# Attention block on one core: P times V for two key tiles in one burst, and side products in slots after each score pair

## The chip, the cores and the metric

One core of a Trainium2 chip runs the whole program. The metric is the device time of one execution in microseconds (us); the kernel before takes 1757.31 us (median of three runs, 1756.65 to 1758.82).

## The reference

A transformer block on 2048 tokens of width 512: attention with 32 query heads of 16 columns that share one key and one value head, then a gated product (GLU without a nonlinearity), both behind a layer norm whose scale and shift come from a condition vector.

```python
mod = (silu(c) @ w_mod).reshape(c.shape[0], 6, 1, -1)        # sa, ca, ga, sb, cb, gb
h = layernorm(x) * (1 + ca) + sa
q = (h @ wq) per head;  k = h @ wk;  v = h @ wv              # 32 heads of q, one of k and v
p = softmax(einsum("bhqd,bkd->bhqk", q, k) * 16 ** -0.5)
x = x + ga * (einsum("bhqk,bkd->bhqd", p, v) @ wo)
h = layernorm(x) * (1 + cb) + sb
x = x + gb * (((h @ w_gate) * (h @ w_up)) @ w_down)          # 512 -> 1792 -> 512
```

## The kernel before

Attention is done in 32 *units*: a unit is four heads for one block of 512 queries (four blocks, eight units each). Keys come in 16 *key tiles* of 128. The loop over a unit has 32 *steps*; step i treats key tile `kt = i // 2` and head pair `p = i % 2`. Everything is issued by hand in program order, so the order in the code is the order in which each engine works.

A step issues two *pairs* on TensorE. A pair is one score product and one row-max product, which use the two halves of the array's rows (64 rows each) at the same time:

- `qk_exp(u, kt, p, a)`: the score product `sc` (L579, fp16) for this unit into a PSUM bank, and the exponential on ScalarE (L581), which writes half a tile `P`. A tile `P` holds the two heads of one key tile and one `p`. `P` has four buffers.
- `max_half(a)`, which calls `max_mm`: the row maxima are needed before a unit starts, so this runs 38 steps ahead, for a later unit: a product `mx` (L542) into a bank, and a maximum over 512 columns on VectorE (L544). The last 38 steps of the loop have none.

At odd steps follows `pv(u, kt - 1)`: P times V for one key tile (L588), four heads into four column groups of 32, all into one PSUM bank `pv`, in fp32, which the chip runs as two passes: eight matmul records in a profile. This is one *burst*. At the first odd step of a unit the last key tile of the unit before is done, and its result is read by ScalarE (`pv_out`, L594).

At even steps *side products* are issued, from a queue `fill`: products of q for later units (`one`: full-array products, L500, two at a time), and the work on the query block that is finished: the product with wo, transposes (`solo`, L713), gate, up and down products (`duo`, L469). A `duo` runs two product groups at once, each on one half of the array's rows; one place in it, two half products side by side, is called a *slot* here. It has two *turns* of as many slots: in the second turn the groups swap halves. After the second turn the results are read (`post`): the first group's at once, the second's at the next `drain_mids`. How many slots an even step takes is set by `pace` (what is left over what is left of the time to `due`), a `credit` that grows with it, and the bounds `BURST` = 6 and `LEAST` = 4: four to six slots, or none.

PSUM has eight banks: three `mx`, two `sc`, one `pv`, one `misc` and one `spare`. `spare` is a third score bank as long as no `duo` runs (`ps_sc`); a `duo` takes `misc` and `spare`.

After the loop the *tail* does what is left of the side products, and the last query block's.

Of the kernel before, what the change touches and what calls it, by code (L numbers as in the profile page):

```python
# [13 lines left out]
F32 = mybir.dt.float32  # L14
# [5 lines left out]
S, D, H, DH, F = 2048, 512, 32, 16, 1792  # L20
# [16 lines left out]
ONE_WAIT = 3  # L37
RESERVE = 31000.0
TR_GAP = 8
BURST = 6  # L40
LEAST = 4
NHF = 14
V_STEP = 31
M_STEP = 25
# [8 lines left out]
def adaln_mqa_glu_kernel(ctx: ExitStack, tc: tile.TileContext, x_in, wq_in, wk_in, wv_in, wo_in,  # L53
# [45 lines left out]
    xbig = big.tile([128, 6, 2, D], F32, name="xbig", tag="wu")  # L99
    xts = [xbig[:, i] for i in range(6)]  # L100
    for i in range(6, 8):
        xts.append(work.tile([128, 2, D], F32, name="P", tag="P", bufs=4))
    for i in range(8):
        if i == 2:
            nc.sync.dma_start(wmA[:, :, 0:1024], wm_v[:, :, 0:1024])
# [468 lines left out]
    def qk_exp(u, kt, p, a):  # L574
        s = sst[u % 3]
        if (u, kt, p) not in ptl:
            ptl[u, kt, p] = work.tile([128, 2, D], F32, name="P", tag="P", bufs=4)
        t = ps_sc()
        nc.tensor.matmul(t, kst[64 * a:64 * a + 50, kt * 128:(kt + 1) * 128],  # L579
                         s[64 * a:64 * a + 50, p, :], start=True, stop=True)  # L580
        nc.scalar.activation(ptl[u, kt, p][:, a, :], t, AF.Exp)  # L581
# [68 lines left out]
    def wo_work(b):  # L650
        def op(t):
            def f(i):
                ch, term = divmod(i, 3)
                ol, wl = TERMS[term]
                return och[b, ch][:, ol, t * 128:(t + 1) * 128], wo[:, wl, ch, :]
            return f

        def pre(t):
            def f(tag=None):
                load_x(b, t)  # L660
                return ps_misc(tag=tag)
            return f

        def fin(t):
            def f(p):
                if b < NB - 1:
                    x1 = work.tile([128, D], F32, name="x1", tag="x1", bufs=4)
                else:
                    x1 = work.tile([128, D], F32, name="x1p", tag="P", bufs=4)
                nc.vector.scalar_tensor_tensor(x1, p, sca[:, 7:8], xls[b, t], op0=OP.mult, op1=OP.add)  # L670
                x1s[b, t] = x1
                s2 = work.tile([128, 1, 2], F32, name="st2", bufs=5)
                bs = work.tile([128, 6], F32, name="bs", bufs=4)
                nb = work.tile([128, 2], F32, name="nb", bufs=4)
                yt = {}

                def spread():
                    nc.vector.bn_stats(bs, x1)

                def aggr():  # L680
                    nc.vector.bn_aggr(s2[:, 0, :], bs)
                    yt["y"] = rstd_of(s2, 1)
                    nc.gpsimd.tensor_tensor(nb[:, 0:1], s2[:, 0, 0:1], yt["y"], op=OP.mult)
                    nc.gpsimd.tensor_scalar(nb[:, 1:2], nb[:, 0:1], -1.0, 0.0, op0=OP.mult, op1=OP.add)

                def nrm():
                    n2 = work.tile([128, D], F32, name="n2", tag="och", bufs=4)
                    nc.scalar.activation(n2, x1, AF.Identity, bias=nb[:, 1:2], scale=yt["y"])
# [329 lines left out]
    def pace(step):  # L1018
# [7 lines left out]
            most = max(most, (n - kept) / max((due - step) / 2, 1.0))  # L1026
        return most

    def open_gate(step):
        if not fill or (fill[0][1] == "one" and step < cur["wait"]):  # L1030
            return False
        if fill[0][1] == "duo" and NU * NSTEP - step < 2 * -(-fill[0][2][0].n // BURST) + 2:
# [6 lines left out]
    def fill_gap(step):  # L1039


        if cur["gen"] is None:
            if not open_gate(step):
                return
            _, kind, what, due = fill.popleft()
            if kind == "solo":
                _, f, post = what
                credit[0] -= 4.0
                f()
                if post:  # L1050
                    posts.append(post)
                return
            if kind == "one":
                cur.update(gen=plain(what), left=what.n, turn=what.n, second=True, due=due, swapped=-9, one=True)
            else:
                begin(step, what, due)
        if cur["one"]:
            burst(step, max(1, min(int(credit[0]), cur["left"], MOST_ONE)))
            return
        turn = cur["turn"]  # L1060
        parts = max(-(-turn // BURST), min(round(turn / max(credit[0], 1.0)), turn // LEAST), 1)
        n = -(-turn // parts)
        if not cur["second"]:
            n = max(n, -(-cur["turn"] // max((NU * NSTEP - 2 - step) // 2, 1)))
        burst(step, n)

    def begin(step, two, due, tags=("misc", "spare")):
        cur.update(gen=duo(*two, tags=tags), left=2 * two[0].n, turn=two[0].n, second=False, due=due, swapped=-9,
                   one=False)

    def burst(step, n):
        for _ in range(n):
            swap = next(cur["gen"], None)
            credit[0] -= 1.0
            cur["left"] -= 1
            cur["turn"] -= 1
            if swap is None:
                cur["gen"], cur["left"], cur["wait"] = None, 0, step + ONE_WAIT
                return
            if swap:  # L1080
                cur["turn"], cur["second"], cur["swapped"] = cur["left"], True, step
                return

    side = deque(wlist)
# [45 lines left out]
    for u in range(NU):  # L1130
# [3 lines left out]
        for i in range(NSTEP):  # L1134
# [3 lines left out]
            spare["scores"] = not spare["held"] and (cur["gen"] is None or cur["one"]) and not (fill and fill[0][1] == "duo" and open_gate(step))  # L1138
            max_half(0)
            qk_exp(u, kt, p, 1)  # L1140
            drain_mids()
            qk_exp(u, kt, p, 0)
            max_half(1)
            if p == 1:
                if kt == 0:
                    if u > 0:
                        pv(u - 1, KT - 1)
                        posts.append(lambda u=u: pv_out(u - 1))
                else:
# [30 lines left out]

    u = NU - 1

    pv(u, KT - 1)
    pv_out(u)
    left = cur["left"]
    if cur["gen"] is not None:
        assert cur["second"] and NU * NSTEP - cur["swapped"] > 2
        for _ in cur["gen"]:
            drain_posts()
        drain_mids()  # L1190
# [51 lines left out]
```

## Time and profile before

| What | Value |
|---|---|
| Runs | 1756.65, 1757.31, 1758.82 us |
| Span of the profiled execution | 1754.7 us |
| TensorE busy | 1695.0 us, 97% |
| VectorE busy | 1412.2 us, 80% |
| ScalarE busy | 1220.7 us, 70% |
| GpSimd (POOL) busy | 505.0 us, 29% |
| Row maxima on VectorE (L544) | 2048, 682 ns each |
| Exponentials on ScalarE (L581) | 2048, 596 ns each |
| P times V matmul records (L588) | 4096, from 95.9 to 1603.3 us |

The profiled execution's time outside its span isn't listed; the runs' median is 2.6 us above the span. A row of the timeline gives the start in us from the span's start, the length, engine, line, operation, what it writes and reads, and how many are merged (`x2`); in brackets stands the idle time before it and what ended it. Matmuls are pipelined: a record is longer than its share of TensorE, and the distance between starts tells what one costs. In a group's row stand busy time and mean length, then the engine's idle time before, with its releaser.

### The profile page before, as it was taken

The numbers are of one execution on the slowest core, as the hardware profiler recorded it, in microseconds if no ns is written. First come the engines' busy times: TensorE is split into PE (matmuls) and PEld (weight loads), VectorE is DVE, ScalarE is ACT, GpSimd is POOL, SyncE is SP. The second block draws the span as 40 slices with busy tenths as digits, with TensorE's granted clock in tenths as the row PEclk, the third lists the DMA queues.
The fourth block names the chain that finished last, engine by engine and source line by source line (L and its number), as shares of the span: only waits on it lengthen the run. The fifth ranks groups of instructions, "written<-read, shape, count | busy, mean of one in ns | idle before, by whom it ended". The sixth has DMA issues, their size and how long they took to land.

```text
span 1754.7 us, 32145 instructions
## 1 busy us (share of the span) xinstructions
PE 1695.0 (97%) x12655; PEld 540.8 (31%) x12655; DVE 1412.2 (80%) x2363; ACT 1220.7 (70%) x2277; POOL 505.0 (29%) x703
## 2 busy tenths in 40 slices
PE   6899899999999999999999999999999999999999
PEld 3222222222223333333223333333223333324444
DVE  7899899999988888888988888888998899920310
ACT  3478788888777777777787777777787777774210
POOL 5714344646576741100031011100031010110330
PEclk9999999999989999999999999999999999999999
DMA  5202121212222200000100000000100000001000
GB/s 197 101 30 85 52 79 55 89 38 91 81 62 60 69 22 9 5 15 19 41 19 16 9 16 9 5 15 18 51 9 16 9 16 9 11 4 41 19 1 24
DMA packets 48899, 66.58 MB, mean 38 GB/s; under 512 B 15270, under 2 KB 29418, under 8 KB 48748
## 3 DMA queue, kind: packets, MB, share of 16 engines
q1 hardware_dynamic: 47164, 64.33, 11.9%
q8 instruction: 99, 1.62, 0.4%
q14 instruction: 52, 0.43, 0.1%
q10 hardware_dynamic: 1584, 0.20, 0.1%
HBM read 51.12 MB, written 8.92 MB: 34 GB/s over the span
## 4 chain that ended last, share of the span: by engine, by line
PE 83%; ACT 7%; DVE 3%; POOL 3%; DMA 2%; issue 1%; SPq 1%; ACTq 0%; POOLq 0%; DVEq 0%
PE pv L588 27%; PE misc L469 18%; PE mx L542 14%; PE sc L579 13%; PE misc L500 9%; ACT P L581 5%; DVE mpart L544 2%; ACT ev L594 1%; POOL h L395 1%; DMA wmA<-in_w_mod_dram 1%; DMA wsl<-in_B_w_gate_dram 0%; ACT qf L510 0%; DVE x L670 0%; PE mxt L556 0%; PE misc L252 0%
## 5 line engine op out<-in xcount | busy, mean ns | idle before, releaser
L544 DVE TENSOR_REDUCE mpart<-mx 128x1 f32<-128x512 f32 x2048 | 1296.1, 682 | 135.8 <-PE sc L579 117.3
L581 ACT ACTIVATE P<-sc 128x512 f32<-128x512 f32 x2048 | 1102.2, 596 | 320.8 <-PE sc L579 311.7
L542 PE MATMUL mx<-kst,sst 48*128 48x512 f16 x2048 | 649.7, 385 | 15.3 <-DVE mpart L544 12.2
L579 PE MATMUL sc<-sst,kst 50*128 50x512 f16 x2048 | 631.7, 383 | 20.9 <-ACT P L581 17.6
L588 PE MATMUL pv<-P,vst 128*32 128x512 f32 x4096 | 552.0, 611 | 0.0
L542 PEld LDWEIGHTS <-sst 48*128 48x128 f16 x2048 | 156.0, 94 | 574.9 <-issue 519.2
L469 PE MATMUL misc<-h2T,wu 64*128 64x512 f16 x1008 | 253.5, 375 | 0.0
L469 PE MATMUL misc<-h2T,wg 64*128 64x512 f16 x1008 | 253.5, 375 | 0.0
L763 POOL TENSOR_SCALAR glu<-gf 128x512 f16<-128x512 f32 x56 | 34.7, 620 | 544.7 <-DVE gf L762 544.7
L579 PEld LDWEIGHTS <-kst 50*128 50x128 f16 x2048 | 138.3, 94 | 80.1 <-issue 40.5
L588 PEld LDWEIGHTS pv<-P,vst 128*32 128x32 f32 x4096 | 81.1, 108 | 173.6 <-issue 168.5
L469 PEld LDWEIGHTS <-wu 64*128 64x128 f16 x1008 | 94.6, 94 | 57.5
L469 PEld LDWEIGHTS <-wg 64*128 64x128 f16 x1008 | 94.3, 94 | 52.4 <-issue 0.9
L762 DVE TENSOR_TENSOR gf<-misc,g 128x512 f32<-128x512 f32 x56 | 38.2, 683 | 86.8 <-PE misc L500 62.9
L469 PE MATMUL misc<-wd,glu 64*128 64x512 f16 x840 | 105.8, 375 | 0.0
L621 POOL TENSOR_TENSOR oc<-oc,rr 128x512 f32<-128x512 f32 x15 | 19.1, 1277 | 257.7 <-DMA sst<-qd 154.2
L756 ACT ACTIVATE g<-misc 128x512 f32<-128x512 f32 x56 | 33.5, 598 | 69.1 <-PE misc L500 63.4
L764 POOL TENSOR_TENSOR glu<-gf,glu 128x512 f16<-128x512 f32 x56 | 64.8, 1157 | 4.7
L469 PEld LDWEIGHTS <-glu 64*128 64x128 f16 x840 | 43.6, 94 | 45.7 <-issue 1.7
L500 PE MATMUL misc<-wd,glu 128*128 128x512 f16 x252 | 55.1, 379 | 0.0
L500 PE MATMUL misc<-h,wq 128*128 128x512 f16 x168 | 51.2, 387 | 0.0
L848 POOL TENSOR_TENSOR kwb<-kwb,wsl 128x448 f32<-128x448 f32 (+1 forms) x40 | 47.5, 1188 | 3.1
(230 smaller groups left out, 886.7 us busy)
## 6 DMA issues: line engine op xcount, KB each, us to landing
wsl<-in_B_w_gate_dram SPq DMA_DIRECT2D x32, 224.0 KB
wsl<-in_B_w_up_dram SPq DMA_DIRECT2D x32, 224.0 KB
wsl<-in_B_w_down_dram SPq DMA_DIRECT2D x28, 256.0 KB
sst<-qd SPq DMA_DIRECT2D x186, 32.0 KB
qd<-q SPq DMA_DIRECT2D x16, 256.0 KB
oc<-ev SPq DMA_DIRECT2D x128, 32.0 KB
rr<-ri SPq DMA_DIRECT2D x16, 256.0 KB
xl<-in_A_x_dram SPq DMA_DIRECT2D x16, 256.0 KB
```

The source lines that it names most:

```text
L469: nc.tensor.matmul(p, left[64 * r:64 * r + 64], right[64 * r:64 * r + 64], start=start, stop=stop)
L500: nc.tensor.matmul(p, left, right, start=i == 0, stop=i == g.n - 1)
L542: nc.tensor.matmul(m, s[64 * a:64 * a + 48, p, t * 128:(t + 1) * 128], kst[64 * a:64 * a + 48, kc * 512:(kc + 1) * 512], start=True, stop= ...
L544: nc.vector.tensor_reduce(mparts[u][:, a, p, t, kc:kc + 1], m, axis=AX.X, op=OP.max)
L579: nc.tensor.matmul(t, kst[64 * a:64 * a + 50, kt * 128:(kt + 1) * 128], s[64 * a:64 * a + 50, p, :], start=True, stop=True)
L581: nc.scalar.activation(ptl[u, kt, p][:, a, :], t, AF.Exp)
L588: nc.tensor.matmul(pvb[u][32 * j:32 * j + 32, :], vst[:, kt, :], ptl[u, kt, p][:, a, :], start=(kt == 0), stop=(kt == KT - 1))
L756: nc.scalar.activation(st["g", f], p, AF.Copy, scale=2.0 ** -45)
L762: nc.vector.tensor_tensor(gf, p, st["g", f], op=OP.mult)
L763: nc.gpsimd.tensor_scalar(st["glu"][:, 0, f, :], gf, 1.0, 0.0, op0=OP.mult, op1=OP.add)
L764: nc.gpsimd.tensor_tensor(st["glu"][:, 1, f, :], gf, st["glu"][:, 0, f, :], op=OP.subtract)
L848: nc.gpsimd.tensor_tensor(acc, acc, t, op=OP.add)
```

## The change

- At every fourth step (`i % 4 == 1`) `pv` is called for two key tiles in a row, kt-2 and kt-1; at the first such step of a unit for the last two key tiles of the unit before. Products so start a key tile later, and `P` has six buffers.
- `fill_gap` becomes `fill_slot`, called after each pair except the one ahead of a burst: seven places between two bursts (numbered 0 to 6). `plan` spreads a turn of a `duo` over these places, or over those of several bursts, so that it ends at a burst. A new `duo` begins two steps after the last at the earliest, at one of the first four places. Products of q and transposes are issued at places 1 and 5.
- `drain_mids` (reading the second group's result) moves from the middle of each step to just ahead of a burst.

```diff
-BURST = 6
-LEAST = 4
+SLOTS = 7
+SLOT_MOST = 3
+CREDIT = 9.0
+DUO_WAIT = 2
...
-            ptl[u, kt, p] = work.tile([128, 2, D], F32, name="P", tag="P", bufs=4)
+            ptl[u, kt, p] = work.tile([128, 2, D], F32, name="P", tag="P", bufs=6)
...
+    def plan(step, k):
+        rate = max(2 * pace(step), 1.0)
+        part = (SLOTS - k) / SLOTS
+        n = max(0, round((cur["turn"] - credit[0]) / rate - part))
+        if part < 0.5 and cur["turn"] > SLOT_MOST * (SLOTS - k):
+            n = max(n, 1)
+        last = (END - 3 - step) // 4
+        cur["slots"] = SLOTS - k + SLOTS * (min(n, last) if not cur["second"] else n)
+
+    def fill_slot(step, k):
...
+        if cur["slots"] == 0:
+            if k == 0 or (step - 2) // 4 == (cur["swapped"] - 2) // 4:
+                return
+            plan(step, k)
+        n = cur["turn"] // cur["slots"]
+        cur["slots"] -= 1
         burst(step, n)
...
             qk_exp(u, kt, p, 1)
-            drain_mids()
+            fill_slot(step, 2 * ((i - 2) % 4))
             qk_exp(u, kt, p, 0)
             max_half(1)
-            if p == 1:
-                if kt == 0:
-                    if u > 0:
-                        pv(u - 1, KT - 1)
-                        posts.append(lambda u=u: pv_out(u - 1))
-                else:
+            if i % 4 == 1:
+                drain_mids()
+                if kt > 0:
+                    pv(u, kt - 2)
                     pv(u, kt - 1)
+                elif u > 0:
+                    pv(u - 1, KT - 2)
+                    pv(u - 1, KT - 1)
+                    posts.append(lambda u=u: pv_out(u - 1))
                 late_max()
-            elif fill or cur["gen"]:
-                credit[0] = min(credit[0] + pace(step), 9.0)
-                one = cur["one"] if cur["gen"] else fill[0][1] == "one"
-                if credit[0] >= (MOST_ONE if one else 1.0):
-                    fill_gap(step)
+            else:
+                fill_slot(step, 2 * ((i - 2) % 4) + 1)
```

TensorE's order in unit 7, where no side products run, around a burst (`P` is the tile of exponentials, `sst` the queries, `kst` the keys). Before:

```order
L579 LDWEIGHTS kst_124
L579 MATMUL sc_5361<-sst1_120,kst_124 128x512
L542 LDWEIGHTS sst2_122
L542 MATMUL mx_5364<-kst_124,sst2_122 128x512
L588 MATMUL pv_5187<-P_5301,vst_117 32x512 x2
L588 MATMUL pv_5187<-P_5327,vst_117 32x512 x2
L542 LDWEIGHTS sst2_122
L542 MATMUL mx_5376<-kst_124,sst2_122 128x512
```

and now:

```order
L581 LDWEIGHTS kst_124
L581 MATMUL sc_5357<-sst1_120,kst_124 128x512
L544 LDWEIGHTS sst2_122
L544 MATMUL mx_5360<-kst_124,sst2_122 128x512
L590 MATMUL pv_5231<-P_5276,vst_117 32x512 x2
L590 MATMUL pv_5231<-P_5289,vst_117 32x512 x2
L590 MATMUL pv_5231<-P_5310,vst_117 32x512 x2
L590 MATMUL pv_5231<-P_5327,vst_117 32x512 x2
L544 LDWEIGHTS sst2_122
L544 MATMUL mx_5376<-kst_124,sst2_122 128x512
```

The burst has eight products (sixteen passes) in place of four, and eight pairs stand between two bursts in place of four.

TensorE's order in unit 14, where `duo` slots of the down product run (`misc` are their two banks, `glu` and `wd` their operands). Before, the last of four slots and the two pairs behind it:

```order
L469 LDWEIGHTS glu_6883
L469 MATMUL misc_10046<-wd_7426,glu_6883 128x512
L469 LDWEIGHTS glu_6883
L469 MATMUL misc_10045<-wd_7426,glu_6883 128x512
L542 LDWEIGHTS sst1_120
L542 MATMUL mx_10555<-kst_124,sst1_120 128x512
L579 LDWEIGHTS kst_124
L579 MATMUL sc_10559<-sst2_122,kst_124 128x512
L579 LDWEIGHTS kst_124
L579 MATMUL sc_10562<-sst2_122,kst_124 128x512
L542 LDWEIGHTS sst1_120
L542 MATMUL mx_10565<-kst_124,sst1_120 128x512
```

and now:

```order
L471 LDWEIGHTS glu_7036
L471 MATMUL misc_10085<-wd_7370,glu_7036 128x512
L471 LDWEIGHTS glu_7036
L471 MATMUL misc_10084<-wd_7370,glu_7036 128x512
L581 LDWEIGHTS kst_124
L581 MATMUL sc_10557<-sst2_122,kst_124 128x512
L544 LDWEIGHTS sst1_120
L544 MATMUL mx_10560<-kst_124,sst1_120 128x512
L471 LDWEIGHTS glu_7036
L471 MATMUL misc_10085<-wd_7370,glu_7036 128x512
L471 LDWEIGHTS glu_7036
L471 MATMUL misc_10084<-wd_7370,glu_7036 128x512
```

One slot now stands between pair and pair, where four stood between pairs two and three. Counted over the whole order, between the first burst of the loop and the last:

| Side products between two bursts | before: 511 short groups (4 pairs, 1 key tile) | after: 255 long groups (8 pairs, 2 key tiles) |
|---|---|---|
| no slots, no products of q (transposes and weight sums included) | 90 | 36 |
| no slots, products of q (2; after: 2 or 4) | 84 | 49 |
| slots | 202 with 4, 46 with 5, 69 with 6 | 35 with 5, 4 with 6, 39 with 7, 4 with 8, 4 with 9, 62 with 12, 12 with 14 |
| without row maxima (end of the loop) | 9 with 4, 9 with 6, 2 with none | 2 each with none, 5 and 7; one each with 12, 15, 27, 42 |

After the loop stand 666 side products and slots before, 636 now.

More of the change, by code (lines that the diff above doesn't have):

```diff
@@ L101, in adaln_mqa_glu_kernel @@
     for i in range(6, 8):
-        xts.append(work.tile([128, 2, D], F32, name="P", tag="P", bufs=4))
+        xts.append(work.tile([128, 2, D], F32, name="P", tag="P", bufs=6))
     for i in range(8):
@@ L668, in f @@
                 else:
-                    x1 = work.tile([128, D], F32, name="x1p", tag="P", bufs=4)
+                    x1 = work.tile([128, D], F32, name="x1p", tag="P", bufs=6)
                 nc.vector.scalar_tensor_tensor(x1, p, sca[:, 7:8], xls[b, t], op0=OP.mult, op1=OP.add)
@@ L1027, in pace @@
         return most
+    END = NU * NSTEP
     def open_gate(step):
-        if not fill or (fill[0][1] == "one" and step < cur["wait"]):
-            return False
-        if fill[0][1] == "duo" and NU * NSTEP - step < 2 * -(-fill[0][2][0].n // BURST) + 2:
+        if not fill or step < cur["wait"]:
             return False
@@ L1037, in open_gate @@
         return gate[0] <= step
-    def fill_gap(step):
+    def plan(step, k):
[7 more added lines that the diff above has]
+    def fill_slot(step, k):
+        if k == 0 and (cur["gen"] or fill) and not cur["one"]:
+            credit[0] = min(credit[0] + 2 * pace(step), CREDIT)
         if cur["gen"] is None:
@@ L1044, in fill_gap @@
                 return
-            _, kind, what, due = fill.popleft()
+            _, kind, what, due = fill[0]
+            if kind != "duo":
+                credit[0] = 0.0
+                if k % 4 != 1:
+                    return
+            elif k > 3 or END - step < 7:
+                return
+            fill.popleft()
             if kind == "solo":
                 _, f, post = what
-                credit[0] -= 4.0
                 f()
@@ L1056, in fill_gap @@
                 begin(step, what, due)
+                plan(step, k)
         if cur["one"]:
-            burst(step, max(1, min(int(credit[0]), cur["left"], MOST_ONE)))
+            if k % 4 == 1:
+                burst(step, min(cur["left"], MOST_ONE))
             return
[L1060 to L1064, printed above, removed]
+        if cur["slots"] == 0:
+            if k == 0 or (step - 2) // 4 == (cur["swapped"] - 2) // 4:
+                return
+            plan(step, k)
+        n = cur["turn"] // cur["slots"]
+        cur["slots"] -= 1
         burst(step, n)
     def begin(step, two, due, tags=("misc", "spare")):
+        spare["scores"] = False
         cur.update(gen=duo(*two, tags=tags), left=2 * two[0].n, turn=two[0].n, second=False, due=due, swapped=-9,
@@ L1073, in burst @@
             swap = next(cur["gen"], None)
-            credit[0] -= 1.0
+            credit[0] = max(credit[0] - 1.0, -4 * CREDIT)
             cur["left"] -= 1
@@ L1077, in burst @@
             if swap is None:
-                cur["gen"], cur["left"], cur["wait"] = None, 0, step + ONE_WAIT
+                cur["gen"], cur["left"], cur["wait"] = None, 0, step + (ONE_WAIT if cur["one"] else DUO_WAIT)
                 return
             if swap:
-                cur["turn"], cur["second"], cur["swapped"] = cur["left"], True, step
+                cur["turn"], cur["second"], cur["swapped"], cur["slots"] = cur["left"], True, step, 0
                 return
@@ L1181, in adaln_mqa_glu_kernel @@
     u = NU - 1
+    pv(u, KT - 2)
     pv(u, KT - 1)
@@ L1186, in adaln_mqa_glu_kernel @@
     if cur["gen"] is not None:
-        assert cur["second"] and NU * NSTEP - cur["swapped"] > 2
+        assert cur["second"] and END - 2 > cur["swapped"]
         for _ in cur["gen"]:
```

## The prediction

> **What bounds the kernel now.** I read the page's first part, the costliest groups and the chain first.
>
> ```profile
> span 1754.7 us, 32145 instructions
> PE 1695.0 (97%) x12655; PEld 540.8 (31%) x12655; DVE 1412.2 (80%) x2363; ACT 1220.7 (70%) x2277; POOL 505.0 (29%) x703
> PE 83%; ACT 7%; DVE 3%; POOL 3%; DMA 2%; issue 1%; SPq 1%; ACTq 0%; POOLq 0%; DVEq 0%
> L544 DVE TENSOR_REDUCE mpart<-mx 128x1 f32<-128x512 f32 x2048 | 1296.1, 682 | 135.8 <-PE sc L579 117.3
> L581 ACT ACTIVATE P<-sc 128x512 f32<-128x512 f32 x2048 | 1102.2, 596 | 320.8 <-PE sc L579 311.7
> ```
>
> By this TensorE is all. But PE's busy time counts matmuls that overlap, so I went to the order of time. I call a "pair" one row-max product (mx, L542) beside one score product (sc, L579), on the two halves of the array's rows; a "burst" the P times V products (L588); a "short group" what lies from one burst's start to the next in before: four pairs, a burst of one key tile, perhaps side products. Unit 7, without side products, from three engines' timelines (start, length):
>
> ```profile
> 417.48 6.89 DVE L544 TENSOR_REDUCE mpart<-mx 128x1 f32<-128x512 f32 x11
> 418.32 0.39 PE L542 MATMUL mx<-kst,sst 48*128 48x512 f16 x1
> 418.78 2.07 ACT L581 ACTIVATE P<-sc 128x512 f32<-128x512 f32 x4 [0.41 <-PE sc L579]
> 419.43 0.37 PE L579 MATMUL sc<-sst,kst 50*128 50x512 f16 x1 [0.22 <-ACT P L581]
> 419.49 0.37 PE L542 MATMUL mx<-kst,sst 48*128 48x512 f16 x1
> 419.79 1.07 PE L588 MATMUL pv<-P,vst 128*32 128x512 f32 x8
> 420.79 0.39 PE L542 MATMUL mx<-kst,sst 48*128 48x512 f16 x1
> ```
>
> First pair to first pair is 2.47 us. Here TensorE waits: VectorE runs eleven reductions without a gap, 0.62 each by start ((6.89-0.68)/10), four to a group, 2.48. The fourth mx starts 1.17 after the first, when reduction one has given its bank back (there are three). The burst, 0.30 later and 1.00 long, is covered: VectorE meanwhile eats the three full banks.
>
> Unit 11, with four side slots (L469; a slot is two half products side by side):
>
> ```profile
> 608.53 0.39 PE L542 MATMUL mx<-kst,sst 48*128 48x512 f16 x1
> 608.95 2.59 DVE L544 TENSOR_REDUCE mpart<-mx 128x1 f32<-128x512 f32 x4 [0.32 <-PE sc L579]
> 608.98 1.08 ACT L581 ACTIVATE P<-sc 128x512 f32<-128x512 f32 x2 [0.53 <-PE sc L579]
> 609.84 0.38 PE L542 MATMUL mx<-kst,sst 48*128 48x512 f16 x1
> 610.12 0.39 PE L542 MATMUL mx<-kst,sst 48*128 48x512 f16 x1
> 610.44 1.07 PE L588 MATMUL pv<-P,vst 128*32 128x512 f32 x8
> 611.44 0.39 PE L542 MATMUL mx<-kst,sst 48*128 48x512 f16 x1
> ```
>
> The group is 2.91. Pairs and slots follow each other by 0.218 (608.53 to 609.84 is six steps); the last pair comes 0.28 after its neighbour, not 0.22, because its score bank (two while side products hold the spare one) is read by an exponential until 608.98+1.08=610.06. So here TensorE is almost, and the bank just, the bound. With two full-array products (first two rows) the group is 2.61, with six slots (next two) 3.27, both TensorE's own sum; without row maxima, at the end, 2.86:
>
> ```profile
> 339.47 1.06 PE L588 MATMUL pv<-P,vst 128*32 128x512 f32 x8
> 342.08 0.64 PE L588 MATMUL pv<-P,vst 128*32 128x512 f32 x4
> 601.35 1.07 PE L588 MATMUL pv<-P,vst 128*32 128x512 f32 x8
> 604.62 0.64 PE L588 MATMUL pv<-P,vst 128*32 128x512 f32 x4
> 1569.44 1.06 PE L588 MATMUL pv<-P,vst 128*32 128x512 f32 x8
> 1572.30 1.06 PE L588 MATMUL pv<-P,vst 128*32 128x512 f32 x8
> ```
>
> **What the bursts cost, and what merging saves.** From a pair into a burst takes 0.32 (610.12 to 610.44) and out of one 1.00-0.45=0.55, where the same steps without a change of the array's layout take 0.22 and 0.43. The 0.43 and 0.45 come from the program's end, where two bursts already stand together:
>
> ```profile
> 1601.71 0.64 PE L588 MATMUL pv<-P,vst 128*32 128x512 f32 x4
> 1602.16 1.03 PE L588 MATMUL pv<-P,vst 128*32 128x512 f32 x6
> 1603.78 2.55 PE L469 MATMUL misc<-wd,glu 64*128 64x512 f16 x22
> L588 PE MATMUL pv<-P,vst x4096: 592/617/1062, 95.9 to 1603.3; 128*32 128x512 f32 x196
> ```
>
> Pass two starts 0.45 after pass one; pass three, of the next key tile, 1.03-0.59-0.01=0.43 later. A burst of two key tiles is thus 0.45+0.43+0.43+0.55=1.86 against 2.00 for two. Bounds: 1.72 if the exit too cost no more than a pass, 2.00 if nothing is saved; 1.86 is nearest to the row. The second burst of that row began late (the last products wait for an exponential), so its end, 1603.78, is no price. In TensorE's sum each merge saves 0.32+0.55-0.22-0.43=0.22.
>
> The Trainium skill, "TensorEngine Tiling (Array Packing)", Key Properties, says that changing the tiling mode drains TensorE; the extra 0.10 before and 0.12 after each burst agree. If that drain were all, the change would win; that is the first rival.
>
> **What the longer burst costs elsewhere.** From the last pair to the first pair after it no bank is filled: 0.32+1.86=2.18 instead of 1.32. I work out a "long group" (eight pairs, burst of two; four steps) from those rows.
>
> *Without side slots:* the mx banks are still three. The fourth mx can start at 1.17, each later one 0.62 after, so the eighth at 1.17+4x0.62=3.65; the burst at 3.95; the next group at 3.95+1.86=5.81. At the eighth mx VectorE has three reductions left, which end at about 3.60+3x0.62=5.46; the next can start 0.42 after its mx (608.53 to 608.95), at 6.23, so VectorE stands 0.77 idle where before it never waited. Two short groups are 4.94 without, 5.22 with products of q, two of which take 2.61-1.00-0.32-2x0.22=0.85; in a long group TensorE's sum with them, 1.86+0.32+5x0.22+2x0.85=4.98, stays under 5.81. I take 5.80; with 0.60 for a reduction it is 5.73.
>
> *With five to nine slots:* the score banks are two, and the exponentials' chain decides. The fourth score can start at 1.57 (610.10, after exponential two). Each later use of that bank waits for score to exponential 0.45 (608.53 to 608.98), its 0.59, and 0.05: 1.09. The eighth score starts at 1.57+2x1.09=3.75, the burst 0.34 later, the next group at 5.95. TensorE's own sum would be 1.86+0.32+(7+n)x0.218, 4.80 for five and 5.23 for seven, so up to 1.1 us of TensorE stand idle. Two short groups with four slots each are 5.83.
>
> *With twelve:* TensorE's sum, 2.18+19x0.218=6.32 (fourteen: 6.76); the spread slots keep the scores 0.65 apart, so neither bank is late. Two short groups with six each are 6.54: here the merge wins its 0.22.
>
> The skill speaks against the change too: "Perfetto Trace Analysis", Optimization Strategy, takes consistent bubbles for a sign that there is too little PSUM for the next tile. The row 419.43 with its wait is such a bubble; by that rule the long burst needs more mx and sc banks, and it gets none. That is what I take.
>
> **The sum.** The last row above gives the loop of before: bursts start from 95.9 to 1602.6 (its last key tile's first pass), 1506.7 us. By the counts in the section on the change, short groups make 90x2.47+84x2.61+202x2.91+46x3.05+69x3.27=1396, and the last 20 without row maxima 55: 1451. The remaining 55 are waits at unit borders, transposes and weight sums. Long groups: 85x5.80=493, 86x5.95=512, 62x6.32=392, 12x6.76=81, and the last ten 68 (two without slots 8.6, four of five or seven 23.6, then 12, 15, 27 and 42 slots at TensorE's sum 6.3, 7.0, 9.5, 12.7): 1546. Of the 55 I keep 40, since some of it waits for POOL, whose pace is not the loop's:
>
> ```profile
> PEld mx L858 <- POOL kwb L848: 5.4, 2, 4.3
> PE mx L858 <- POOL kwb L848: 5.0, 2, 4.1
> ACT n L688 <- POOL nb L684: 6.7, 4, 2.8
> ```
>
> The bounds for that are 0 and 55. The first burst comes two steps later, +2.5; 30 slots more are done in the loop than before, so the tail loses 30x0.216=6.5. Together 1546+40-1506.7+2.5-6.5=+75.
>
> The other parts. Six buffers of P in place of four: no instruction; the exponential that reuses a buffer waits for products one burst back, done about 1 us earlier, so nothing. One key tile later: the exponentials read are two steps old in both. The reading of a side result, moved by "a turn ends at P times V", takes ScalarE 0.60 and VectorE 0.68 for two turns,
>
> ```profile
> L756 ACT ACTIVATE g<-misc 128x512 f32<-128x512 f32 x56 | 33.5, 598 | 69.1 <-PE misc L500 63.4
> L762 DVE TENSOR_TENSOR gf<-misc,g 128x512 f32<-128x512 f32 x56 | 38.2, 683 | 86.8 <-PE misc L500 62.9
> ```
>
> and falls into the idle time under the burst (0.77 on VectorE, more on ScalarE): hidden there, and were that cover gone it would cost up to 56x0.7=39. Where it was in the way before, it is part of the 15 us I let go. Products of q come in the same twos, some groups earlier; with them move their SyncE stores and two POOL instructions each, among weight loads which that queue issues with slack. SyncE has the same transfers as before, and POOL is 29% busy.
>
> The profile's span 1754.7 becomes 1829.5; the runs' median, 1757.3, lies 2.6 above the span, so I say 1832.
>
> **Rivals.**
> 1. *Faster: TensorE stays the bound.* 97% and 83% of the chain speak for it, the twelve-slot groups too. 255 merges x 0.22=-56: 1701. It decides if pairs could be issued ahead of the banks; against it stand the 0.22 wait at 419.43 and the late 610.12, which show banks as the limit already under a burst half as long.
> 2. *About the same.* The plain groups lose as priced, but the slots between pairs let exponentials and reductions keep up, so that the 86 groups of five to nine run at TensorE's own sum (35 of five, 39 of seven, 12 around them: 436 instead of 512): 1756. For it: in before the groups with four slots missed TensorE's sum by only 0.06. Against: the chain of 3.75 has no slot in it, and VectorE's 5.81 holds there too.
> 3. *Slower still: the merged burst breaks.* If the second key tile's products don't follow on, as in the row of 1601.71 to 1603.78 (2.07), 0.21x255=+54: 1886. Against: its exponentials are two steps old, there they were a few tenths of a microsecond old.
>
> **Chances.** Forecast 0.85, rival 1 0.08, rival 2 0.04, rival 3 0.03. Bounds of the sum: burst 1.72 to 2.00, -36 to +36; reductions, -6; waits kept, -40 to +15. They add up only in part: 1786 to 1866 leaves each end one of its two large terms in full. The rivals outside are 0.15 together, the ends of the forecast itself a few hundredths more. Faster by over 0.2% (about what a measurement here can tell from none) 0.08, within it 0.04, slower 0.88.
>
> **What would show it.** In the changed profile: bursts of sixteen passes with 1.86 to the next mx; in units 1 to 7 a gap of about 0.8 before the first reduction after each burst, with no counterpart in before, and groups of 5.8; in units 26 to 29 groups of 5.95 with late scores beside groups of 6.3; VectorE's share falling to 77%, with its busy time unchanged. I am wrong if groups without slots take 5.2 or less, or if VectorE shows no new idle time.

## The result, and the profile after

The changed kernel takes 1900.1 us (median of four runs, 1898.4 to 1905.8), the kernel before 1757.3 beside it: 1.0822 times as long, 95% interval 1.0800 to 1.0843. The sign of the forecast holds, its size doesn't: +75 were forecast (1832, range 1786 to 1866), +143 came. The profiled execution is the longest of the four, 1905.8 with a span of 1904.0; so the sums below, which come from it, hold some 5 us more than the median.

From the page of after: span, busy times, the clock by slices, and the two groups that read the banks.

```profile
span 1904.0 us, 32149 instructions
PE 1788.9 (94%) x12655; PEld 603.0 (32%) x12655; DVE 1391.8 (73%) x2363; ACT 1218.3 (64%) x2277; POOL 503.4 (26%) x703
PEclk9989899998898999999989999999999999999999
L546 DVE TENSOR_REDUCE mpart<-mx 128x1 f32<-128x512 f32 x2048 | 1271.3, 681 | 258.8 <-PE sc L581 232.3
L583 ACT ACTIVATE P<-sc 128x512 f32<-128x512 f32 x2048 | 1103.4, 599 | 405.4 <-PE sc L581 386.7
```

No engine got more to do; both readers of the banks stand idle longer, VectorE ahead of its reductions 258.8 us in place of 135.8, ScalarE 405.4 in place of 320.8. TensorE's busy time grew by 94 us with the same 12655 matmuls: part of that is the clock, whose row has six eights where before's has one (PEclk is given in tenths of full speed).

Unit 7 of after, without side products, on TensorE, and below on VectorE (468 to 478 us):

```profile
473.27 1.92 PE L590 MATMUL pv<-P,vst 128*32 128x512 f32 x16
475.13 0.39 PE L544 MATMUL mx<-kst,sst 48*128 48x512 f16 x1
...
476.24 0.37 PE L581 MATMUL sc<-sst,kst 50*128 50x512 f16 x1 [0.28 <-ACT P L583]
...
476.90 0.37 PE L544 MATMUL mx<-kst,sst 48*128 48x512 f16 x1 [0.23 <-DVE mpart L546]
...
478.09 0.37 PE L544 MATMUL mx<-kst,sst 48*128 48x512 f16 x1 [0.22 <-DVE mpart L546]
...
478.99 3.34 PE L590 MATMUL pv<-P,vst 128*32 128x512 f32 x16
482.26 0.61 PE L544 MATMUL mx<-kst,sst 48*128 48x512 f16 x1
```

```profile
469.84 4.87 DVE L546 TENSOR_REDUCE mpart<-mx 128x1 f32<-128x512 f32 x8 [2.49 <-PE sc L581]
475.55 3.08 DVE L546 TENSOR_REDUCE mpart<-mx 128x1 f32<-128x512 f32 x5 [0.84 <-PE sc L581]
```

Two things are to be seen. The group from 473.27 to 478.99 is 5.72, its burst 1.86 up to the next mx, and VectorE stands 0.84 idle behind it: the mechanism of the forecast, to 0.1 us. Of the 255 bursts 218 take just this 1.86. And the next burst, of the same sixteen passes, takes 3.34 instead of 1.92: TensorE runs there at half clock (0.5 granted from 479.4 to 482.8), and VectorE's wait grows to about 2.5 (as in the first VectorE row, after such a burst). That was in no term of the sum.

I grouped TensorE's records from burst to burst and added the lengths by what lies between (the groups of the table in the section on the change). The measured column holds the waits that the forecast kept as a lump of 40:

| Long groups | forecast us | after us | mean each, forecast and after |
|---|---|---|---|
| 85 without slots | 493 | 547.4 | 5.80, 6.44 (shortest 5.72) |
| 86 with 5 to 9 slots | 512 | 527.4 | 5.95, 6.13 (shortest 5.89) |
| 62 with 12 | 392 | 425.8 | 6.32, 6.87 |
| 12 with 14 | 81 | 80.9 | 6.76, 6.74 |
| last ten | 68 | 69.5 | |
| waits kept | 40 | in the rows above | |
| loop | 1586 | 1651.1 | |

The profiled execution's span is 74.5 us above the 1829.5 forecast for it. 65 of them lie in the loop, the rest behind it (7) and ahead of it (2). Three places stand out.

*Twelve slots.* One such group in unit 12:

```profile
748.79 1.92 PE L590 MATMUL pv<-P,vst 128*32 128x512 f32 x16
750.65 0.39 PE L544 MATMUL mx<-kst,sst 48*128 48x512 f16 x1
750.65 0.60 PE L581 MATMUL sc<-sst,kst 50*128 50x512 f16 x2
...
751.75 0.37 PE L581 MATMUL sc<-sst,kst 50*128 50x512 f16 x1 [0.28 <-ACT P L583]
...
755.75 0.64 PE L590 MATMUL pv<-P,vst 128*32 128x512 f32 x4
```

It is 6.96 long, not 6.32. Two scores go out together at 750.65, with no slot between; the third has to wait for the first exponential, until 1.10 after, and all slots wait behind it.

*Row-max transposes.* A group with seven slots that begins with `mxt` (L558), which `late_max` issues once per unit, and the rows of the waits that name its transfer (us in total, times, longest):

```profile
761.64 1.92 PE L590 MATMUL pv<-P,vst 128*32 128x512 f32 x16
763.49 0.28 PE L558 MATMUL mxt<-ident,mm 128*16 128x128 f32 x1
...
766.48 0.37 PE L581 MATMUL sc<-sst,kst 50*128 50x512 f16 x1 [0.38 <-DMA sst<-mt]
...
768.35 1.06 PE L590 MATMUL pv<-P,vst 128*32 128x512 f32 x8
```

```profile
PEld L581 <- DMA sst<-mt: 26.9, 26, 2.1
PE sc L581 <- DMA sst<-mt: 11.7, 28, 1.3
```

The group takes 6.71, its neighbours without a transpose 5.89. The row maxima, transposed at 763.49, have to be in the next unit's queries by a transfer, and it holds that unit's first score until 766.48. Before has no such rows among its waits: there `late_max` ran at step 27 of a unit, five steps ahead of the next. As the last line of the burst's branch it now runs at step 29.

*The clock.* From the first burst to the last, the stretches at a granted clock of 0.5, each 3.41 us long or up to four times that, add up to 99 us; in before to 32. All of before's and 86 of the 99 lie in groups without slots.

### The profile page after: what moved, and what is told of

Read it like the earlier page. It is cut to its first block, busy times and chain, and to the rows that moved or that the text cites. A ratio compares the mean times of both kernels' runs of the same rounds, so it can differ in the third digit from the quotient of the medians.

```text
span 1904.0 us, 32149 instructions
## 1 busy us (share of the span) xinstructions
PE 1788.9 (94%) x12655; PEld 603.0 (32%) x12655; DVE 1391.8 (73%) x2363; ACT 1218.3 (64%) x2277; POOL 503.4 (26%) x703
## 5 line engine op out<-in xcount | busy, mean ns | idle before, releaser
L546 DVE TENSOR_REDUCE mpart<-mx 128x1 f32<-128x512 f32 x2048 | 1271.3, 681 | 258.8 <-PE sc L581 232.3
L583 ACT ACTIVATE P<-sc 128x512 f32<-128x512 f32 x2048 | 1103.4, 599 | 405.4 <-PE sc L581 386.7
L581 PE MATMUL sc<-sst,kst 50*128 50x512 f16 x2048 | 715.1, 382 | 58.2 <-ACT P L583 40.5
L544 PE MATMUL mx<-kst,sst 48*128 48x512 f16 x2048 | 720.8, 385 | 27.8 <-DVE mpart L546 20.6
L590 PE MATMUL pv<-P,vst 128*32 128x512 f32 x4096 | 529.4, 637 | 0.0
L471 PE MATMUL misc<-h2T,wg 64*128 64x512 f16 x1008 | 323.8, 376 | 2.2 <-ACT hf L722 2.2
L471 PE MATMUL misc<-h2T,wu 64*128 64x512 f16 x1008 | 324.8, 376 | 0.0
L581 PEld LDWEIGHTS <-kst 50*128 50x128 f16 x2048 | 158.5, 94 | 127.6 <-issue 71.3
L590 PEld LDWEIGHTS pv<-P,vst 128*32 128x32 f32 x4096 | 111.3, 113 | 272.8 <-issue 260.5
L471 PE MATMUL misc<-wd,glu 64*128 64x512 f16 x840 | 145.0, 376 | 0.0
L471 PEld LDWEIGHTS <-glu 64*128 64x128 f16 x840 | 43.4, 94 | 52.8 <-issue 20.5
L471 PE MATMUL misc<-wo,och 64*128 64x512 f16 x288 | 51.9, 376 | 0.0
```

The costliest lines, as they stand in the source:

```text
L471: nc.tensor.matmul(p, left[64 * r:64 * r + 64], right[64 * r:64 * r + 64], start=start, stop=stop)
L544: nc.tensor.matmul(m, s[64 * a:64 * a + 48, p, t * 128:(t + 1) * 128], kst[64 * a:64 * a + 48, kc * 512:(kc + 1) * 512], start=True, stop= ...
L546: nc.vector.tensor_reduce(mparts[u][:, a, p, t, kc:kc + 1], m, axis=AX.X, op=OP.max)
L590: nc.tensor.matmul(pvb[u][32 * j:32 * j + 32, :], vst[:, kt, :], ptl[u, kt, p][:, a, :], start=(kt == 0), stop=(kt == KT - 1))
```

## The experiments

Each comparison has runs of before beside it (medians 1754.8 to 1757.0); "after" is the changed kernel's 1900.1.

| Run | us | over before, 95% |
|---|---|---|
| after | 1900.1 | 1.0822 (1.0800 to 1.0843) |
| 1 transposes at every odd step | 1883.1 | 1.0713 (1.0680 to 1.0747) |
| 2 slots as in after, single burst | 1839.1 | 1.0476 (1.0459 to 1.0494) |
| 3 slots as in before, long burst | 1925.2 | 1.0964 (1.0944 to 1.0985) |
| 4 after, reductions halved | 1851.8 | 1.0546 (1.0531 to 1.0562) |
| 5 after, slots further forward | 1868.9 | 1.0632 (1.0613 to 1.0651) |
| 6 after, dummy products | 1880.5 | 1.0698 (1.0682 to 1.0714) |
| 7 = 1 + 5 + 6 | 1835.1 | 1.0445 (1.0430 to 1.0461) |
| 8 after, reductions and exponentials halved | 1736.9 | 0.9883 (0.9867 to 0.9900) |
| 9 before, one dummy product | 1753.4 | 0.9990 (0.9981 to 0.9999) |
| 10 before, two dummy products | 1754.5 | 0.9997 (0.9989 to 1.0006) |
| 11 before, both halved | 1692.3 | 0.9631 (0.9615 to 0.9647) |
| 12 = 7, both halved | 1701.5 | 0.9680 (0.9665 to 0.9694) |

**Run 1: the transposes back at every odd step.**

```diff
-                late_max()
             else:
                 fill_slot(step, 2 * ((i - 2) % 4) + 1)
+            if p == 1:
+                late_max()
```

> The changed kernel with one edit: the rounding-off of the row maxima (late_max: a transpose, two small copies, two DMAs into the query tile) is again called at every odd step, not only at the step of a burst. Theory: in the changed kernel it falls at step 29 of a unit, three steps before the first score that needs it, and 31 groups are 0.8 us longer (6.71 for 5.89) because scores wait for those DMAs; at step 27 the wait is gone, the group costs 0.2 to 0.4 for the transpose in a place of its own, and the time falls by 12 to 20 us, to 1880 to 1888. Rival: the wait is only where another one shows, and the time stays within 3 us of 1900.

17 us came back. A group with seven slots and the transpose in it, on TensorE:

```profile
1001.58 1.92 PE L590 MATMUL pv<-P,vst 128*32 128x512 f32 x16
...
1005.57 0.28 PE L558 MATMUL mxt<-ident,mm 128*16 128x128 f32 x1
...
1007.70 0.64 PE L590 MATMUL pv<-P,vst 128*32 128x512 f32 x4
```

6.12 instead of 6.71, the transpose now in the middle of the group, two steps earlier; the two rows that name `sst<-mt` are gone from the waits. The place of `late_max` is shown as one cause. How much of the 17 us is its wait alone isn't: the half-clock time of the loop fell too, from 99 to 72 us.

**Runs 2 and 3: one half of the change each.** Run 2 keeps the slots and everything else of after, with a burst of one key tile at every odd step; run 3 takes before and changes the burst alone.

```diff
# run 2, against after
-                    pv(u, kt - 2)
                     pv(u, kt - 1)
...
                 fill_slot(step, 2 * ((i - 2) % 4) + 1)
+                if p == 1:
+                    pv(u, kt - 1)
# run 3, against before (and six buffers of P)
-                else:
+                elif kt % 2 == 0:
+                    pv(u, kt - 2)
                     pv(u, kt - 1)
```

> The changed kernel with P times V again for one key tile at every odd step; the slots between pairs, their plan and the six buffers stay. Theory (the long burst starves VectorE and ScalarE of banks): groups without slots fall from 5.72 to about 5.1 for four steps, the half-clock stretches around units 7 and 8 go, VectorE's idle time before a reduction after a burst goes; 1815 to 1835. Rival (the spread of the slots between pairs is what slows TensorE): 1880 or more, groups with twelve slots as slow as before.

> The kernel before with the long burst alone: P times V for two key tiles every fourth step, six buffers of P, all else (slots in fours to sixes at even steps, row maxima at odd steps) as it was. Theory (the long burst): groups of four steps without slots 5.7 in place of 4.9 to 5.2, with four and four slots 5.9 to 6.0 in place of 5.83, half-clock stretches in unit 7; 1840 to 1870. Rival (the slots' order is at fault, the burst saves its 0.22): 1700 to 1760.

| us | burst of one | burst of two | difference |
|---|---|---|---|
| slots four to six in a row | 1755 | 1925 | +170 |
| slots in ones to threes | 1839 | 1900 | +61 |
| difference | +84 | -25 | |

Each half alone loses, and they don't add. The place of `late_max` is in the table too: run 3 calls it as before does, run 2 and after at step 29, where run 2 waits 1.6 us for the transfer on TensorE and after 11.7. So up to 17 of the 61 belong to it. What decides for the slots is where they stand beside the waits. A group of run 2 with four slots:

```profile
621.64 1.06 PE L590 MATMUL pv<-P,vst 128*32 128x512 f32 x8
...
623.74 0.37 PE L581 MATMUL sc<-sst,kst 50*128 50x512 f16 x1
...
624.23 0.37 PE L581 MATMUL sc<-sst,kst 50*128 50x512 f16 x1
...
624.77 0.64 PE L590 MATMUL pv<-P,vst 128*32 128x512 f32 x4
```

It takes 3.13, before's with the same four slots 2.91. The fourth score starts 2.59 after the burst (624.23) in both kernels, since it waits for the second exponential. Before spends that wait on all four slots, in one lump where the third score waits; in run 2 one of the four stands behind the fourth pair, where it delays the next burst by its 0.22. So lumps suit a single burst: over the groups with slots, before sums to 969 us, run 2 to 1048, and that is nearly all of the 84. The run lies 4 us above the range I had given it. A group of run 3 with eight slots:

```profile
536.36 1.92 PE L588 MATMUL pv<-P,vst 128*32 128x512 f32 x16
...
540.62 0.86 PE L579 MATMUL sc<-sst,kst 50*128 50x512 f16 x2 [0.22 <-ACT P L581]
...
542.73 0.64 PE L588 MATMUL pv<-P,vst 128*32 128x512 f32 x4
```

6.37, against twice 2.91 and a sum of TensorE of 2.18+15x0.218=5.45. The lumps stand behind pairs two and six; pairs three to six follow each other with no slot between, and their scores wait for the banks. I had expected the chain of 5.95 there, which is the price of slots spread evenly, and so missed this run by 55 us: its groups with slots sum to 1115. The spreading of the slots is what the long burst needs, and it wins 25 us with it (42 where `late_max` is in its old place, run 1).

**Run 4: reductions over 256 of 512 columns** (row maxima of half the keys; the exponential's argument divided by 16).

```diff
-        nc.vector.tensor_reduce(mparts[u][:, a, p, t, kc:kc + 1], m, axis=AX.X, op=OP.max)
+        nc.vector.tensor_reduce(mparts[u][:, a, p, t, kc:kc + 1], m[:, 0:256], axis=AX.X, op=OP.max)
```

> The changed kernel with the row maximum taken over the first 256 of each 512 columns, so that a reduction lasts about 0.4 us in place of 0.68; half of that work is left out, and the exponential's argument is scaled by 1/16 so that it stays finite. All products and exponentials stay. Theory: groups without slots are bound by VectorE's three banks, so they fall from 5.72 to about 5.3, where ScalarE's three score banks decide; groups of five and seven slots are bound by the two score banks and stay at 5.89; 1840 to 1870 in all. Rival (the burst or ScalarE bounds all groups): no group changes, 1895 to 1905.

Its group of reductions, and a group without slots, from burst to burst:

```profile
L546 DVE TENSOR_REDUCE mpart<-mx 128x1 f32<-128x256 f32 x2048 | 810.2, 421 | 631.3 <-PE sc L581 365.2
```

```profile
101.28 1.93 PE L590 MATMUL pv<-P,vst 128*32 128x512 f32 x16
...
104.25 0.37 PE L581 MATMUL sc<-sst,kst 50*128 50x512 f16 x1 [0.28 <-ACT P L583]
...
106.52 0.64 PE L590 MATMUL pv<-P,vst 128*32 128x512 f32 x4
```

With reductions of 0.42 the group without slots is 5.24, not 5.72, so VectorE set its length; now the exponential does, at 104.25. The shortest groups with five or seven slots stay at 5.89: there VectorE never was the bound, ScalarE's chain is. 48 us of the change's price hang on VectorE's 0.68, what it does to the clock included (47 us at half clock in the loop, not 99).

**Run 5: the slots further forward.** A turn may begin at place 1 of the very next group, not at place 0, and place 1 takes one slot more.

```diff
-DUO_WAIT = 2
+DUO_WAIT = 1
...
-            elif k > 3 or END - step < 7:
+            elif not 0 < k <= 3 or END - step < 7:
...
+        if k == 1:
+            n = min(n + 1, SLOT_MOST, cur["turn"])
```

> The changed kernel with the twelve slots of a turn moved forward: a turn may begin one step after the last, at place 1, and place 1 takes one slot more (three, where twelve go into a group, then 1, 2, 2, 2, 2). Theory: in the changed kernel the third score of a group waits for the first exponential, 1.10 us after the group's first pair, and TensorE has nothing to do until then if only two slots, or none, stand ahead of it; with three the wait is covered, and groups of twelve fall from 6.52 and 6.95 to 6.32 to 6.40; 1872 to 1882 in all. Rival (slots between pairs shift the two row halves against each other, which costs TensorE throughput): groups of twelve stay at 6.5 or more, 1895 to 1905.

A group with twelve slots:

```profile
602.83 1.92 PE L590 MATMUL pv<-P,vst 128*32 128x512 f32 x16
...
605.79 0.37 PE L581 MATMUL sc<-sst,kst 50*128 50x512 f16 x1
...
609.21 0.64 PE L590 MATMUL pv<-P,vst 128*32 128x512 f32 x4
```

6.38: three slots stand between the second pair and the third, and the third score no longer waits. That is near the 6.32 of the forecast; the mean of the twelve-slot groups went from 6.87 to 6.58. 31 us came back, 3 more than I expected at most, and not all from these groups: of the 41 us between the two profiled executions about 18 lie in groups with twelve slots, 9 in those with five to nine and 13 in those without, with the half-clock time of the loop down to 68 us.

**Run 6: dummy products.** At places 1 and 5, where no side product is to be had, two products of keys with keys, whose result nobody reads. They add work to TensorE and to no other engine.

```diff
+    def warm():
+        p = ps_misc(tag="misc")
+        for _ in range(2):
+            nc.tensor.matmul(p, kst[:, 0:128], kst[:, 0:512], start=True, stop=True)
...
+                if k % 4 == 1 and step >= cur["wait"]:
+                    warm()
```

> The changed kernel with two products on the keys that nobody reads at places 1 and 5 of groups that have no side product ready (about 110 added in 38 groups), in the pattern that products of q have in units 1 to 6. Theory: in units 7 to 9 TensorE's idle time makes the clock fall to half again and again, a burst in such a stretch takes 3.3 in place of 1.9, and groups that need 5.72 take 7.1; with the added products the half-clock stretches there go, units 7 and 8 fall from 54.7 and 54.3 to 47 to 49; 1878 to 1888 in all, though work is added. Rival (the time there is VectorE's or a transfer's): no less than 1900.

The same stretch of the clock, 449 to 503 us, in after and in this run (length, busy us and count of TensorE, its weight loads, VectorE, ScalarE, POOL; then the granted clock, the DMA share and GB/s):

```profile
449.00:503.00 54.00, 47.59 (x261) 11.66 (x257) 39.39 (x66) 33.18 (x66) 26.04 (x33) 0.84 0.19 55
```

```profile
449.00:503.00 54.00, 52.40 (x343) 12.14 (x336) 45.50 (x78) 39.71 (x76) 30.63 (x39) 1.00 0.22 64
```

The clock goes from 0.84 to 1.00, and in the same time VectorE gets through 78 operations instead of 66. In the whole loop 40 us at half clock are left of 99. Units 7 and 8 take 46.5 and 49.8 us, in after 54.7 and 54.3. More work on TensorE made the kernel 20 us faster: the clock's share is shown.

**Run 7: runs 1, 5 and 6 together.**

> The changed kernel with three edits together: row maxima rounded off at odd steps, the twelve slots moved forward, and the added products of the run before. Theory: three separate losses, so the gains add, 17 + 22 + 17: 1838 to 1850; what then remains above the kernel before (about 85) is the long burst with too few banks. Rival (the gains overlap): 1865 or more.

17, 31 and 20 are 68; together they give 65. So the three gains add, to within 3 us, though not as three causes wholly apart: runs 1 and 5 had less half clock too, and in run 7 30 us of it are left in the loop. Without the three the change costs what was forecast: 1835.1 against 1832, with a loop of 1584.9 against 1586. Part of so close a match is luck: with run 5's starts the groups hold other numbers of slots than the forecast counted, and groups without slots still take 28 us more than their 493, which is where most of the 40 us of waits lie.

**Runs 8, 11 and 12: reductions and exponentials both over half the columns,** in after, in before and in run 7. P times V reads the 256 exponentials twice, so that TensorE's work stays as it was. The edit, beside that of run 4:

```diff
-        nc.scalar.activation(ptl[u, kt, p][:, a, :], t, AF.Exp)
+        nc.scalar.activation(ptl[u, kt, p][:, a, 0:256], t[:, 0:256], AF.Exp, scale=0.0625)
...
-            nc.tensor.matmul(pvb[u][32 * j:32 * j + 32, :], vst[:, kt, :], ptl[u, kt, p][:, a, :],
+            nc.tensor.matmul(pvb[u][32 * j:32 * j + 32, :].rearrange("p (a n) -> p a n", a=2), vst[:, kt, :], ptl[u, kt, p][:, a, None, 0:256].to_broadcast([128, 2, 256]),
```

> The run with the half row maximum, and the exponential too on the first 256 of 512 columns; P times V reads those 256 twice, so that TensorE's work is the same. Theory: the banks were all that stood between these groups and TensorE's own sum, so groups of five go from 5.89 to 4.8 to 5.1, of seven to 5.2 to 5.4, groups without slots below 5.0; 1690 to 1750 in all, under the kernel before, with the long burst in place. Rival (the long burst or the change of layout bounds them): groups of five and seven stay above 5.7, 1840 to 1852.

> The kernel before, with reductions and exponentials over 256 of 512 columns (P times V reads the 256 twice), as in the run with both halved and the long burst, so that the two can be compared under banks that come free early. Groups of before that waited for VectorE (90 of 2.47) should fall to TensorE's own sum of 1.98, those with four slots from 2.91 to 2.85: some 50 us off, 1700 to 1720, if TensorE's clock stays up. Theory A (with early banks the long burst wins, as TensorE's sum says): this kernel lies above the long burst's 1737. Theory B (the long burst as laid out in this change loses even then, through its late row-max transposes, its turns that begin at place 1 or 2, and the chains that are left): it lies at 1700 to 1720, below it.

> The long burst with the row-max transpose at every odd step, the slots pulled forward and the dummy products, all three, and the same halved reductions and exponentials. Against the run before (single burst, halved): if TensorE's sum were all that is left on both sides, 255 merges of 0.22 would make it 56 faster; the groups with five slots took 5.24 with halved work against a sum of 4.80, so some 86 x 0.4 = 34 of that are still lost, and the dummy products may cost some in groups of 4.4: 1680 to 1715, and 0 to 30 below the single burst. If it lies above the single burst, merging doesn't pay here even with early banks.

With banks that come free early, the loss of 143 shrinks: 1737 against 1692 for before under the same relief, and 1701 with run 7's three edits. So some 100 of the 143 are waits for banks that are read too slowly, and what they drag along. Run 8's groups with five slots come down to 5.24, not to the 4.8 to 5.1 that I expected. And the long burst doesn't win in any of these runs; I had expected it to by up to 30. A twelve-slot group of run 12, from its burst to the next:

```profile
633.19 1.92 PE L590 MATMUL pv<-P,vst 128*32 128x512 f32 x16
...
639.50 1.07 PE L590 MATMUL pv<-P,vst 128*32 128x512 f32 x8
```

6.31, TensorE's sum, where two short groups with six slots take 6.54 in run 11; so do those with eight, 5.45 against twice 2.84. In these the merge brings its 0.22. Groups with seven slots still take 5.45 (median) against a sum of 5.23, with five 5.21 against 4.80. Summed by kind, run 12's groups with slots win some 10 us on run 11's, those without lose 9, and the last ten, into which more slots fall, another 10. Run 11 itself came out 8 us below what I expected: the lumps of before are at TensorE's sum (2.84 with four slots) as soon as the banks come free early. Of the 56 that this sum promised for merging nothing is left over in run 12.

But run 12 also carries run 6's dummy products, and here they cost. A group without slots of run 12, with two dummies at each of two places, and one of run 8, which has none:

```profile
400.86 1.92 PE L590 MATMUL pv<-P,vst 128*32 128x512 f32 x16
...
406.08 1.92 PE L590 MATMUL pv<-P,vst 128*32 128x512 f32 x16
```

```profile
407.94 1.92 PE L590 MATMUL pv<-P,vst 128*32 128x512 f32 x16
...
412.32 0.64 PE L590 MATMUL pv<-P,vst 128*32 128x512 f32 x4
```

5.22 against 4.38. Over the 27 groups that have no other side work the mean is 5.52 in run 12 and 4.92 in run 8 (26 of them), some 16 us, more than the 9 by which run 12 loses to run 11. So whether the long burst would win under early banks without the dummies stays open; no run has that combination.

**Runs 9 and 10: the dummy products in the kernel before,** one or two at each even step that has no side product to issue (34 places); `warm` is that of run 6.

```diff
+            elif cur["gen"] is None and not open_gate(step) and step >= cur["wait"]:
+                warm()
```

> The kernel before, with one product of keys with keys (result unused) at each even step at which no side product is to be had (34 places, most of them in units 7 to 9, 16, 17, 24 and 25). In before the profile shows half-clock stretches there too: the five short groups from 496.2 us take 3.26, 5.41, 3.76, 3.57 and 2.66 and the three from 895.3 us 3.26, 3.76 and 2.89, against 2.66 for their neighbours. Theory (TensorE's clock falls in the groups where it waits for banks, and it costs as in the kernel after): those eight come down by some 8 us, and one product of 0.22 fits into the 0.49 that TensorE has left in a short group of 2.47: 1748 to 1753. Rival (the half clock there is started by the wait of 1 to 1.2 us ahead of it, at 492.4 and 891.4, for a product of q or a row maximum, and dummy products cannot reach into that wait): within 2 us of before.

> As the run before, with two such products at each of the 34 places. Two take 0.44 of the 0.49, and short groups with two products of q take 2.61 in place of 2.47: up to 34 x 0.14 = 5 us are lost again. By the theory 1751 to 1757; by the rival 1759 to 1763.

Unit 9 of before, and the same group in run 9:

```profile
499.49 1.93 PE L588 MATMUL pv<-P,vst 128*32 128x512 f32 x8
...
504.36 0.58 PE L579 MATMUL sc<-sst,kst 50*128 50x512 f16 x1 [1.54 <-ACT P L581]
504.36 0.61 PE L542 MATMUL mx<-kst,sst 48*128 48x512 f16 x1
504.90 1.93 PE L588 MATMUL pv<-P,vst 128*32 128x512 f32 x8
```

```profile
499.03 1.06 PE L588 MATMUL pv<-P,vst 128*32 128x512 f32 x8
...
500.89 0.39 PE L1042 MATMUL misc<-kst 128*128 128x512 f16 x1
...
502.08 1.06 PE L588 MATMUL pv<-P,vst 128*32 128x512 f32 x8
```

5.41 became 3.05. That is the best of them: the five groups from 496.23 took 18.7 us, and take 16.1 in run 9. The half-clock time of the loop fell from 32 us to 12. In the whole it brings 2.6 us, a ratio of 0.9990 whose interval ends at 0.9999: the fastest kernel of this study with its whole computation, by little more than can be measured. It falls between what the theory and the rival had said. Two products are no better than one.

## Why the prediction was right in sign and wrong in size

**Right: the mechanism and its prices at full clock.** Burst to next mx 1.86, as forecast; the shortest groups without slots 5.72 against 5.80, with five to nine 5.89 against 5.95, those with fourteen 6.74 against 6.76; VectorE idle 0.84 per burst against 0.77; nothing to be seen of rival 3, whose bursts would break (218 of 255 take 1.86, and 3 us or more only those at half clock). Rival 1, TensorE stays the bound, falls with run 4 and run 8. Rival 2 falls too: the slots between pairs don't bring the groups of five to nine below 5.89.

**Wrong: the term "With twelve".** I worked out that "the spread slots keep the scores 0.65 apart, so neither bank is late" from an even spread. But `plan` lets a turn begin at place 1 or 2, and the first pairs stand together: the third score was late, by the same rule of 1.09 that I had used for the other groups. 62x6.32=392 were 426. Run 5, which moves those slots forward, brought such groups to 6.38 at best and 6.58 on average and returned 31 us, part of them there. The counts of slots I took from the order; where in the group they stand I left out.

**Wrong: "SyncE has the same transfers as before".** True of their number, not of their time. `late_max` is called behind the burst, so it moved by two steps with the burst, and with it the transpose, two small operations and the transfer that a unit's first score waits for. The forecast had no step for it, so it stood at nothing. TensorE and its weight loads wait 11.7 and 26.9 us for that transfer in after; run 1 has no such rows, and returned 17 us.

**Missing: the clock.** I took every length from groups at full clock, though before's trace had 32 us at half clock in its loop, all in groups without slots. With the waits that the change adds it was 99. Run 6, which fills some of them, returned 20 us. The forecast had no term for it.

**Smaller terms.** The 40 us of waits held, as said under run 7. The tail's -6.5 didn't come: from the last burst to the end are 152.9 us after and 152.1 before; 30 slots less are done in it, but TensorE waits 2.54 us for `och` (L625) at 1771.86, before 0.51, and a half-clock stretch follows. "Products of q hidden" holds: in after 23 groups with four of them and no other side work take 5.72 (median), as the shortest groups without any. The 26 that have no side work at all take 7.16, with much of the half clock in them: beside run 6, a second sign that more work on TensorE made these groups shorter. "P's six buffers cost nothing" can't be told from the sums, and no run isolates it. VectorE's share fell to 73%, below the 77% forecast, because the span is longer. Two sums of the forecast, 1396 and 1546, come to 1395 and 1545 from their printed terms; nothing hangs on that.

The range left out these three because its bounds were all sizes of steps I had. One step was wrong and two were missing, and all three had the same sign.

## What to carry to other kernels

Fewer switches of the array's layout are worth their price only if the engines that empty PSUM can ride through the longer stretch: count the banks against burst length, and work the chain of scores and exponentials pair by pair along the real order, slots where they stand, not by the mean spacing. When a piece of code moves, follow everything called behind it to its last consumer, transfers too. And where a change makes TensorE wait, look up in the trace before what the clock does in places that already wait; a wait can cost twice.

## What the runs showed of the hardware

The half clock doesn't need a long pause. In unit 7 of after the stretch of 3.41 us that begins at 479.4 follows a group in which TensorE's longest waits were 0.28, 0.23 and 0.22 us (the rows above), a few of them per group (a wait is counted here from the end of one record to the start of the next); two such stretches come in every 20.5 us from 445 to 544 us, where there are no side products. The Trainium skill, "TensorE: Matmul & The Clock Gate", Part 1, tells of two states of the clock, half and full, chosen over windows of about 3.4 us; the clock values and the 3.41 agree. The same page of the Trainium skill, under "HAM oscillation", gives as abstract rule that there be no pauses of TensorE over some 3.4 us; by these rows that rule alone isn't enough, since the waits here are about a tenth of it. What share of a window must be busy no run here shows; two dummy products at each of two places of a group of 5.72 were enough to keep the clock at 1.00 through the 54 us of run 6 shown above.
